# A decode step of gated attention and MLP: layer 1 and q with the weights stationary

## The chip, the cores and the metric

The kernel runs on one core of a Trainium2 chip. The metric is the device time of one execution in microseconds (us), given as the median of several runs. Executions of one kernel mostly agree within about 1% here, so differences below that are called equal unless said otherwise. Only runs that the record calls fast are used for ratios and verdicts; the medians given are over all runs of a sitting, the few slow ones included.

## The reference, cut to what matters

One token (D = 576) goes two ways, and a gate mixes the results:

```python
g = sigmoid((x * gate_w).sum(-1))
q = x @ wq                              # 576 -> 32 heads of 128
s = q . k   over the last 4096 keys     # 16 K/V heads, 2 q heads on each
o = softmax(s * 128**-0.5) @ v
a = o @ wo                              # 4096 -> 576
h = gelu(x @ w1 + b1)                   # 576 -> 4608, "layer 1"
b = h @ w2 + b2                         # 4608 -> 576
out = g * a + (1 - g) * b
```

Everything is bf16. There is one token, so every weight and every key and value is used once: 53.6 MB are read from HBM for very little arithmetic. K and V are 16.8 MB each, w1 and w2 5.3 MB each, wq and wo 4.7 MB each.

## The kernel before, where the change and the argument touch it

All large loads are issued in program order on one queue (SyncE's, "SPq" in the profile): w1, wq, eight K pairs (2 MB each, two heads), V pairs 0 to 2, half of w2, V pairs 3 to 7, wo, the rest of w2. K and V pairs share a ring of four buffers; a load into a used buffer waits until its reader is done.

A matmul on TensorE first loads one operand into the array (the stationary one) and then streams the other past it (the moving one). Layer 1 keeps x stationary and streams the weights past it. To place block b of the output on row b, the stationary operand is a window into a zero-padded copy of x. The result is four rows of 1152, which VectorE adds the bias to and TensorE turns into columns:

```python
for k in range(KM):                      # 4 slices of 128 input rows
    for b in range(NB):                  # NB = 4
        for c0, c1, dst in pieces:       # 512 + 512 + 128 columns
            nc.tensor.matmul(dst, lhsT=zx[:, k, 7 - b : 7 - b + NB],
                             rhs=w1_m[:, k, b * FB + c0 : b * FB + c1], ...)
# ... the last 64 input rows likewise
nc.vector.tensor_tensor(out=h_row[:], in0=h_ps, in1=b1_t[:], op=ALU.add)
for j in range(NJ):                      # fp32, a column of 128 from every 9th element
    nc.tensor.matmul(hacc[:, j * NB : (j + 1) * NB], lhsT=h_row[:, j:FB:NJ], rhs=ident_f[0:NB, 0:NB], ...)
# ... gelu on 128 x 36
```

q is done alike (36 matmuls of 512 columns, a cast, four transposing matmuls), then copied into the block-diagonal tile `qz`. Then comes the K loop, which the argument is about:

```python
for i in range(NPAIR):
    k_t = load_pair(A_k_cache, i)            # 4 buffers
    for c1 in range(2):
        kt = early[:, c1 * W : (c1 + 1) * W] # one half for each c1: the next pair's transpose
        nc.vector.transpose(out=kt..., in_=k_t[:, c1 * W : (c1 + 1) * W]...)  # frees k_t
        for j in range(4):
            for n in range(2):               # scores: need qz, free kt
                nc.tensor.matmul(s_ps[:, c1, n], lhsT=qz[:, i, j, :], rhs=kv[...], ...)
```

The transposes of pair 0 need no q. Those of pair 1 write where pair 0 lies, so they wait for pair 0's score matmuls, and those need q. The end of the kernel adds 64 half-rows of wo and 36 of w2 into one output row (`y_add`, two matmuls of 288 columns for each row; another 36 matmuls for the first half of w2 run earlier).

## Time and profile before

| | kernel before |
|---|---|
| median of the first 3 runs | 143.1 us |
| span of the profiled execution | 142.7 us |
| HBM read, mean over the span | 53.6 MB, 376 GB/s |
| TensorE matmul busy, VectorE busy | 72%, 37% |

The profiled run of the kernel before is slow (144.51 us), by a small margin.

In the profile PE stands for TensorE's matmuls, PEld for its weight loads, DVE for VectorE, ACT for ScalarE and POOL for GpSimd. The page's strips show the span in 40 slices of 3.57 us: VectorE's busy share in tenths, the share of the DMA engines, and the GB/s they moved.

```profile
...
DVE  3071003040049599999999476500000000100001
...
DMA  5999999999997398999999999999999999999600
GB/s 160 416 430 403 450 432 408 460 409 422 422 436 317 83 427 298 441 390 404 402 422 432 432 420 422 434 427 427 422 427 432 418 438 422 418 418 400 237 3 0
```

The stream moves about 425 GB/s in nearly every slice; it falls in the 13th, 14th and 16th slice and at the end. VectorE is mostly idle before the 13th slice (from 43 us) and nearly full after it. At 425 GB/s, 53.6 MB take 126 us, so a kernel with no hole in its stream would take 126 us and its two ends.

The same hole in the windows view (each row a stretch in us, then its length, busy time of the engines with instruction counts, the TensorE clock that the profile says was granted as a share of full speed, DMA share, GB/s):

```profile
...
core 0: us, PE busy (x) PEld busy (x) DVE busy (x) ACT busy (x) POOL busy (x), PEclk, DMA share, GB/s
...
46.00:48.00 2.00, 2.00 (x6) 0.72 (x5) 1.37 (x1) 0.00 (x0) 0.00 (x0) 0.50 0.04 16
48.00:50.00 2.00, 2.00 (x9) 0.81 (x8) 1.20 (x1) 0.00 (x0) 0.00 (x0) 0.82 0.71 147
54.00:56.00 2.00, 1.71 (x9) 0.67 (x8) 2.00 (x2) 0.00 (x0) 0.00 (x0) 1.00 0.66 197
44.00:68.00 24.00, 20.07 (x79) 7.93 (x79) 22.57 (x11) 0.00 (x0) 0.00 (x0) 0.93 0.84 330
...
```

From 44 to 68 us the mean is 330 GB/s. Against 425 that is 24 x (1 - 330/425) = 5.4 us lost. The waits of the DMA queue say who held it (us in total, number, longest):

```profile
...
engine line waited for: us in total, times, longest us
SPq L312 <- DVE early L333: 41.1, 8, 14.3
...
```

The longest of these waits, 14.3 us, is that of the fifth K load, the first one that needs a used buffer. It is issued here (start, length):

```profile
...
47.40 0.53 SPq L312 DMA_DIRECT2D kv_t<-in_A_k_cache_dram  x1
```

Why so late is in the timeline (start and length in us, engine, line, operation, count; in brackets the idle time before it and what ended it):

```profile
...
start us, us, engine line op out<-in xcount [idle before <-releaser]
...
23.72 1.35 DVE L221 TENSOR_TENSOR h_row<-hq_ps,b_t 4x1152 f32<-4x1152 f32 x1 [12.37 <-PE hq_ps L212]
...
25.12 4.45 PE L225 MATMUL hacc<-ident_f,h_row 4*128 4x4 f32 x18 [1.44 <-DVE h_row L221]
...
29.51 9.80 PE L260 MATMUL hq_ps<-wq_t,zx 128*8 128x512 bf16 x32
...
40.21 0.68 DVE L276 CAST q_r<-hq_ps 8x512 bf16<-8x512 f32 x1 [8.54 <-PE hq_ps L268]
...
42.87 4.51 DVE L333 STREAM_TRANSPOSE early<-kv_t 128x2048 f32<-128x2048 f32 x2
...
45.23 5.10 PE L339 MATMUL s_ps<-early 128*128 128x512 bf16 x15 [1.99 <-DVE early L333]
...
```

VectorE adds layer 1's bias at 23.7 us (L221), TensorE turns the rows (L225, 4.45 us), then streams q's weights (L260, 9.8 us), VectorE casts q at 40.2, and the first K transpose starts at 42.87, with no idle time before it. The first K pair had been in its buffer since about 33 us.

### The profile page before, as it was taken

The page shows a single profiled execution, that of the slowest core. Times are in us where ns is not written, and L with a number is a line of the kernel's source. Part 1 is how long each engine was busy: PE and PEld are TensorE (multiplying, and loading weights), DVE is VectorE, ACT ScalarE, POOL GpSimd, SP SyncE. Part 2 cuts the span into 40 slices and gives each one's busy share as a digit, 9 for nine tenths or more (in the row PEclk, how much of TensorE's full clock was granted, in tenths as well). Part 3 has the DMA queues.
Part 4 walks back from the last instruction along what each step waited for, and adds up shares of the span by engine and source line. Part 5 has one row for each costly group of instructions (what it writes and reads, how often), then busy time and mean ns, then how long its engine had stood idle before and what let it go on. Part 6 is the DMA issues. An engine that isn't in the chain of part 4 may idle for free.

```text
span 142.7 us, 2055 instructions
## 1 busy us (share of the span) xinstructions
PE 103.4 (72%) x922; PEld 56.0 (39%) x922; DVE 52.2 (37%) x71; ACT 6.8 (5%) x11; POOL 2.8 (2%) x13
## 2 busy tenths in 40 slices
PE   1049996999974979888898732999955055099992
PEld 1021342943421323333333212975745045055661
DVE  3071003040049599999999476500000000100001
ACT  3500000000000000000000006000000000000001
POOL 7000000000000000000000000000000000000000
PEclk9999999955998699999999995555995555556999
DMA  5999999999997398999999999999999999999600
GB/s 160 416 430 403 450 432 408 460 409 422 422 436 317 83 427 298 441 390 404 402 422 432 432 420 422 434 427 427 422 427 432 418 438 422 418 418 400 237 3 0
DMA packets 4344, 53.75 MB, mean 377 GB/s; under 512 B 488, under 2 KB 492, under 8 KB 1136
## 3 DMA queue, kind: packets, MB, share of 16 engines
q1 hardware_dynamic: 4322, 53.61, 90.4%
q8 instruction: 7, 0.11, 0.3%
q10 hardware_dynamic: 14, 0.01, 0.0%
q14 instruction: 1, 0.01, 0.0%
HBM read 53.62 MB, written 0.00 MB: 376 GB/s over the span
## 4 chain that ended last, share of the span: by engine, by line
PE 25%; DVE 24%; DMA 14%; issue 2%; ACT 1%; SPq 0%; DVEq 0%
DVE early L333 20%; DMA wo_t<-in_A_wo_dram 14%; PE ya_ps L190 8%; PE yb_ps L191 8%; PE o_ps L423 4%; PE s_ps L339 4%; DVE pt L381 2%; DVE m_466 L351 2%; ACT early L373 1%; PE t_ps L393 1%; SPq L312 0%; DVE mh L360 0%; PE mt_ps L356 0%; ACT out_row L459 0%; PE mb_ps L364 0%
## 5 line engine op out<-in xcount | busy, mean ns | idle before, releaser
L339 PE MATMUL s_ps<-early 128*128 128x512 bf16 x128 | 31.9, 393 | 6.5 <-DVE early L333 6.5
L333 DVE STREAM_TRANSPOSE early<-kv_t 128x2048 f32<-128x2048 f32 x16 | 35.3, 2278 | 1.5 <-PE s_ps L339 1.4
L423 PE MATMUL o_ps<-pt,kv_t 128*128 128x4 bf16 x512 | 14.8, 166 | 13.2 <-DMA kv_t<-in_A_v_cache_dram 10.2
L339 PEld LDWEIGHTS <-early 128*128 128x128 bf16 x128 | 12.6, 98 | 25.7 <-issue 12.8
L423 PEld LDWEIGHTS <-kv_t 128*128 128x128 bf16 x512 | 14.6, 103 | 13.8 <-DMA kv_t<-in_A_v_cache_dram 10.6
L202 PE MATMUL hq_ps<-w_t,zx 128*4 128x512 bf16 (+1 forms) x48 | 11.4, 405 | 6.1 <-DMA w_t<-in_B_w_dram 6.1
L190 PE MATMUL ya_ps<-wo_t,ov 128*1 128x288 bf16 x32 | 10.3, 346 | 3.0 <-DMA wo_t<-in_A_wo_dram 3.0
L190 PE MATMUL ya_ps<-w_t,gt 128*1 128x288 bf16 x36 | 11.0, 333 | 0.0
L191 PE MATMUL yb_ps<-w_t,gt 128*1 128x288 bf16 x36 | 11.0, 333 | 0.0
L442 DVE TENSOR_TENSOR om<-o_ps,rh 128x128 bf16<-128x128 f32 x1 | 0.3, 291 | 28.8 <-PE o_ps L423 28.8
L191 PE MATMUL yb_ps<-wo_t,ov 128*1 128x288 bf16 x32 | 10.3, 345 | 0.0
L260 PE MATMUL hq_ps<-wq_t,zx 128*8 128x512 bf16 x32 | 9.8, 482 | 0.0
L458 DVE CAST out_row<-ya_ps 1x288 bf16<-1x288 f32 x1 | 0.4, 446 | 18.0 <-PE ya_ps L190 18.0
L202 PEld LDWEIGHTS <-zx 128*4 128x4 bf16 x48 | 4.2, 99 | 6.8 <-issue 4.2
L221 DVE TENSOR_TENSOR h_row<-hq_ps,b_t 4x1152 f32<-4x1152 f32 x1 | 1.3, 1346 | 12.4 <-PE hq_ps L212 12.4
L260 PEld LDWEIGHTS <-zx 128*8 128x8 bf16 x32 | 3.3, 105 | 6.0 <-issue 3.8
L225 PE MATMUL hacc<-ident_f,h_row 4*128 4x4 f32 x18 | 4.5, 376 | 1.4 <-DVE h_row L221 1.4
L225 PEld LDWEIGHTS hacc<-ident_f,h_row 4*128 4x128 f32 x18 | 4.4, 330 | 1.8 <-DVE h_row L221 1.8
L191 PEld LDWEIGHTS <-ov 128*1 128x1 bf16 x32 | 3.2, 100 | 4.8 <-issue 2.7
L190 PEld LDWEIGHTS <-gt 128*1 128x1 bf16 x36 | 3.5, 97 | 2.2
L191 PEld LDWEIGHTS <-gt 128*1 128x1 bf16 x36 | 3.4, 96 | 2.2
L373 ACT ACTIVATE early<-s_ps,negm 128x1024 bf16<-128x1024 f32 x2 | 2.2, 1108 | 42.7 <-DVE negm L368 42.7
(88 smaller groups left out, 42.1 us busy)
## 6 DMA issues: line engine op xcount, KB each, us to landing
kv_t<-in_A_k_cache_dram SPq DMA_DIRECT2D x8, 2048.0 KB, 9.0
kv_t<-in_A_v_cache_dram SPq DMA_DIRECT2D x8, 2048.0 KB, 17.1
w_t<-in_B_w_dram SPq DMA_DIRECT2D x2, 2304.0 KB, 10.7
wo_t<-in_A_wo_dram SPq DMA_DIRECT2D x2, 2304.0 KB, 25.5
wq_t<-in_A_wq_dram SPq DMA_DIRECT2D x2, 2048.0 KB, 18.6
w_t<-in_B_w_dram SPq DMA_DIRECT2D x3, 1296.0 KB, 16.9
w_t<-in_B_w_dram SPq DMA_DIRECT2D x2, 576.0 KB, 21.6
wq_t<-in_A_wq_dram SPq DMA_DIRECT2D x1, 512.0 KB, 18.0
```

Source lines behind the costliest of these rows:

```text
L190: nc.tensor.matmul(ya_ps[:], lhsT=vec, rhs=row[:, 0:NH], start=start, stop=stop, skip_group_check=True)
L191: nc.tensor.matmul(yb_ps[:], lhsT=vec, rhs=row[:, NH:D], start=start, stop=stop, skip_group_check=True)
L202: nc.tensor.matmul(dst, lhsT=zx[:, k, 7 - b : 7 - b + NB], rhs=w1_m[:, k, b * FB + c0 : b * FB + c1], start=(k == 0 and b == 0), stop=Fals ...
L225: nc.tensor.matmul(hacc[:, j * NB : (j + 1) * NB], lhsT=h_row[:, j:FB:NJ], rhs=ident_f[0:NB, 0:NB], start=True, stop=True,)
L260: nc.tensor.matmul(q_ps, lhsT=zx[:, k, 7 - m : 7 - m + NQ], rhs=wq_m[:, k, m * 512 : (m + 1) * 512], start=(k == 0 and m == 0), stop=False,)
L333: nc.vector.transpose(out=kt.bitcast(FP32), in_=k_t[:, c1 * W : (c1 + 1) * W].bitcast(FP32))
L339: nc.tensor.matmul(s_ps[:, c1, n], lhsT=qz[:, i, j, :], rhs=kv[:, n, :, j // 2, :, j % 2], start=False, stop=(i == NPAIR - 1 and j == 3), ...
L351: nc.vector.reduce_max(out=m2[:, c1 : c1 + 1], in_=s_ps[:, c1].rearrange("p n k -> p (n k)"), axis=AX.X)
L373: nc.scalar.activation(out=p_x[:, c1 * 1024 : (c1 + 1) * 1024], in_=s_ps[:, c1].rearrange("p n k -> p (n k)"), func=ACT.Exp, bias=negm[:, ...
L381: nc.vector.transpose(out=pt[:, c1 * NCH : (c1 + 1) * NCH, :].rearrange("p c h -> p (c h)"), in_=p_x[:, c1 * 1024 : (c1 + 1) * 1024],)
L393: nc.tensor.matmul(t_ps[:], lhsT=ones_f[:], rhs=sl[:, c1, :], start=(c1 == 0), stop=(c1 == 1))
L423: nc.tensor.matmul(o_ps[:, 4 * i : 4 * i + 4], lhsT=v_t[:, c, :], rhs=pt[:, c, 4 * i : 4 * i + 4], start=(c == 0), stop=(c == 2 * NCH - 1),)
```

## The change

The intent: with one token the matmuls have one column of useful work. Let the weights be the stationary operand, 128 columns a load, and let x move, one column. Outputs then arrive as columns, which is the form that the rest needs: no transposing matmuls, no zero-padded copies, and the bias is added by VectorE on 128 x 36 instead of 4 x 1152 elements. To keep each w2 load's rows long, feature f = block, partition, j maps as before, with two blocks of 18 instead of four of 9, so layer 1's weight load takes every 18th column. w1 arrives in four pieces, whose rows are 9 KB, instead of two of 18 KB, and the first half of w2 in one load instead of two.

```diff
-    NB = 4
+    NB = 2
...
-    b1_t = const.tile([NB, FB], BF16, name="b1_t")
+    b1_t = const.tile([P, NB, NJ], BF16, name="b1_t")
...
-    for k in range(0, KM, 2):
-        nc.sync.dma_start(out=w1_m[:, k : k + 2, :], in_=w1_src[:, k : k + 2, :])
+    for k in range(KM):
+        nc.sync.dma_start(out=w1_m[:, k, :], in_=w1_src[:, k, :])
...
-    (layer 1 as above: 48 + 6 streaming matmuls, bias on rows, 9 fp32 transposing matmuls)
+    h_ps = ps_s.tile([P, NF], FP32, name="h_ps", tag="s")
+    for k in range(KM):
+        for c in range(NF):                       # NF = 36
+            f0 = (c // NJ) * FB + c % NJ
+            nc.tensor.matmul(
+                h_ps[:, c : c + 1],
+                lhsT=w1_m[:, k, f0 : (c // NJ + 1) * FB : NJ],   # NJ = 18
+                rhs=xt[:, k : k + 1],
+                ...
+            )
+    (the last 64 input rows: 18 matmuls of two columns)
+    nc.vector.tensor_tensor(out=hx[:], in0=h_ps[:], in1=b1_t[...], op=ALU.add)
...
-    (q as above: 32 + 4 streaming matmuls, cast, 4 transposing matmuls)
+    for k in range(KM):
+        for j in range(Hq):
+            nc.tensor.matmul(q_ps[:, j : j + 1], lhsT=wq_m[:, k, j * Dh : (j + 1) * Dh],
+                             rhs=xt[:, k : k + 1], ...)
+    (the last 64 input rows: 16 matmuls of two columns)
```

Above, lines in round brackets stand for code that is cut.

More of the change, by code (lines that the diff above doesn't have):

```diff
@@ L67 @@
     nc.scalar.dma_start(out=b2_row[:], in_=B_b2.rearrange("(o n) -> o n", o=1))
-    b1_t = const.tile([NB, FB], BF16, name="b1_t")
-    nc.scalar.dma_start(out=b1_t[:], in_=B_b1.rearrange("(o n) -> o n", o=NB))
+    b1_t = const.tile([P, NB, NJ], BF16, name="b1_t")
+    nc.scalar.dma_start(out=b1_t[:], in_=B_b1.rearrange("(b p j) -> p b j", b=NB, j=NJ))
     w1_t = big.tile([P, KM * F + FH], BF16, name="w1_t", tag="B")
@@ L144 @@
     )
-    zx = const.tile([P, KM, 15], BF16, name="zx")
-    nc.vector.memset(zx[:], 0.0)
-    zq = const.tile([P, 11], BF16, name="zq")
-    nc.vector.memset(zq[:], 0.0)
-    zh = const.tile([P, 5], BF16, name="zh")
-    nc.vector.memset(zh[:], 0.0)
-    nc.vector.tensor_copy(out=zx[:, :, 7], in_=xt_ps[:, 0:KM])
-    nc.vector.tensor_tensor(out=zq[:, 3:8:4], in0=xt_ps[:, 4:6], in1=par[:], op=ALU.mult)
-    nc.vector.tensor_copy(out=zh[:, 1:4:2], in_=zq[:, 3:8:4])
+    xt = const.tile([P, KM], BF16, name="xt")
+    nc.vector.tensor_copy(out=xt[:], in_=xt_ps[:, 0:KM])
+    xl = const.tile([P, 2], BF16, name="xl")
+    nc.vector.tensor_tensor(out=xl[:], in0=xt_ps[:, 4:6], in1=par[:], op=ALU.mult)
     junk_row = const.tile([1, D], BF16, name="junk_row")
@@ L193 @@
     y_add(one_f[0:1, 0:1], b2g[0:1, :], start=True)
-    hq_ps = ps_s.tile([P, 2048], FP32, name="hq_ps", tag="s")
-    h_ps = hq_ps[0:NB, 0:FB]
-    pieces = [(c0, min(c0 + 512, FB), h_ps[:, c0 : min(c0 + 512, FB)]) for c0 in range(0, FB, 512)]
+    h_ps = ps_s.tile([P, NF], FP32, name="h_ps", tag="s")
     for k in range(KM):
-        for b in range(NB):
-            for c0, c1, dst in pieces:
-                nc.tensor.matmul(
-                    dst,
-                    lhsT=zx[:, k, 7 - b : 7 - b + NB],
-                    rhs=w1_m[:, k, b * FB + c0 : b * FB + c1],
-                    start=(k == 0 and b == 0),
-                    stop=False,
-                    skip_group_check=True,
-                )
-    for b in range(NB // 2):
-        for c0, c1, dst in pieces:
-            nc.tensor.matmul(
-                dst,
-                lhsT=zh[:, 1 - b : 1 - b + NB],
-                rhs=w1_l[:, b * FB + c0 : b * FB + c1],
-                start=False,
-                stop=(b == NB // 2 - 1),
+        for c in range(NF):
+            f0 = (c // NJ) * FB + c % NJ
+            nc.tensor.matmul(
+                h_ps[:, c : c + 1],
+                lhsT=w1_m[:, k, f0 : (c // NJ + 1) * FB : NJ],
+                rhs=xt[:, k : k + 1],
+                start=(k == 0 and c == 0),
+                stop=False,
                 skip_group_check=True,
             )
-    h_row = const.tile([NB, FB], FP32, name="h_row")
-    nc.vector.tensor_tensor(out=h_row[:], in0=h_ps, in1=b1_t[:], op=ALU.add)
-    hacc = ps_o.tile([P, NF], FP32, name="hacc", tag="o")
     for j in range(NJ):
         nc.tensor.matmul(
-            hacc[:, j * NB : (j + 1) * NB],
-            lhsT=h_row[:, j:FB:NJ],
-            rhs=ident_f[0:NB, 0:NB],
-            start=True,
-            stop=True,
+            h_ps[:, j:NF:NJ],
+            lhsT=w1_l[:, j:FB:NJ],
+            rhs=xl[:, 0:2],
+            start=False,
+            stop=(j == NJ - 1),
+            skip_group_check=True,
         )
@@ L233 @@
     hx = const.tile([P, NF], FP32, name="hx")
-    nc.vector.tensor_copy(out=hx[:], in_=hacc[:])
+    nc.vector.tensor_tensor(
+        out=hx[:], in0=h_ps[:], in1=b1_t[:].rearrange("p b j -> p (b j)"), op=ALU.add
+    )
     z2 = const.tile([P, NF], FP32, name="z2")
@@ L244 @@
     nc.vector.reciprocal(out=e_h[:], in_=e_h[:])
-    gt = const.tile([P, NJ, NB], BF16, name="gt")
+    gt = const.tile([P, NF], BF16, name="gt")
     nc.vector.scalar_tensor_tensor(
-        out=gt[:].rearrange("p j b -> p (j b)"),
-        in0=hx[:],
-        scalar=omg[:, 0:1],
-        in1=e_h[:],
-        op0=ALU.mult,
-        op1=ALU.mult,
-    )
-    NQ = 8
-    q_ps = hq_ps[0:NQ, 1536:2048]
+        out=gt[:], in0=hx[:], scalar=omg[:, 0:1], in1=e_h[:], op0=ALU.mult, op1=ALU.mult
+    )
+    q_ps = ps_m.tile([P, Hq], FP32, name="q_ps", tag="m")
     for k in range(KM):
-        for m in range(NQ):
+        for j in range(Hq):
             nc.tensor.matmul(
-                q_ps,
-                lhsT=zx[:, k, 7 - m : 7 - m + NQ],
-                rhs=wq_m[:, k, m * 512 : (m + 1) * 512],
-                start=(k == 0 and m == 0),
+                q_ps[:, j : j + 1],
+                lhsT=wq_m[:, k, j * Dh : (j + 1) * Dh],
+                rhs=xt[:, k : k + 1],
+                start=(k == 0 and j == 0),
                 stop=False,
+                skip_group_check=True,
             )
-    for m in range(NQ // 2):
+    for j in range(Hq // 2):
         nc.tensor.matmul(
-            q_ps,
-            lhsT=zq[:, 3 - m : 3 - m + NQ],
-            rhs=wq_l[:, m * 512 : (m + 1) * 512],
+            q_ps[:, j : Hq : Hq // 2],
+            lhsT=wq_l[:, j * Dh : (j + 1) * Dh],
+            rhs=xl[:, 0:2],
             start=False,
-            stop=(m == NQ // 2 - 1),
-        )
-    q_r = const.tile([NQ, 512], BF16, name="q_r")
-    nc.vector.tensor_copy(out=q_r[:], in_=q_ps)
-    qt_ps = ps_m.tile([P, 4, NQ], FP32, name="qt_ps", tag="m")
-    for i in range(4):
-        nc.tensor.matmul(
-            qt_ps[:, i, :],
-            lhsT=q_r[:, i * Dh : (i + 1) * Dh],
-            rhs=ident[0:NQ, 0:NQ],
-            start=True,
-            stop=True,
+            stop=(j == Hq // 2 - 1),
+            skip_group_check=True,
         )
     q_b = const.tile([P, Hq], BF16, name="q_b")
-    nc.vector.tensor_copy(
-        out=q_b[:].rearrange("p (m i) -> p i m", i=4), in_=qt_ps[:]
-    )
+    nc.vector.tensor_copy(out=q_b[:], in_=q_ps[:])
     qj_ps = ps_o.tile([P, 4, NPAIR, 4], FP32, name="qj_ps", tag="o")
@@ L412, in y_w2 @@
         for j in range(NJ):
-            y_add(gt[:, j, b : b + 1], w2_t[:, b, j, :], stop=(b == NB - 1 and j == NJ - 1))
+            y_add(gt[:, b * NJ + j : b * NJ + j + 1], w2_t[:, b, j, :], stop=(b == NB - 1 and j == NJ - 1))
     for i in range(NPAIR):
         if i == 3:
-            for b in range(2):
-                load_w2(b, 0, NJ)
-            for b in range(2):
-                y_w2(b)
+            load_w2(0, 0, NJ)
+            y_w2(0)
         v_t = load_pair(A_v_cache, i)[:].rearrange("p (c d) -> p c d", d=Dh)
@@ L436 @@
         nc.sync.dma_start(out=wo_t[:, r : r + 16, :], in_=wo_src[:, r : r + 16, :])
-    for b, j0, j1 in [(2, 0, 9), (3, 0, 4), (3, 4, 7), (3, 7, 9)]:
+    for b, j0, j1 in [(1, 0, 9), (1, 9, 13), (1, 13, 16), (1, 16, NJ)]:
         load_w2(b, j0, j1)
@@ L453 @@
         y_add(ov[:, r : r + 1], wo_t[:, r, :])
-    for b in range(2, NB):
-        y_w2(b)
+    y_w2(1)
     out_row = const.tile([1, D], BF16, name="out_row")
```

## The prediction

> **What bounds it now.** The DMA stream. Median 143.1 us, profiled span 142.7; 53.6 MB are read. In the windows table the stream moves about 425 GB/s nearly everywhere (53.6 MB at 425 is 126 us). It stops once: from 45 us the one-microsecond windows show 180, 33, 0, 213, 82 GB/s; 54 to 56 us show 164 and 229. Against 425 GB/s that loses 4.9 us (45:56), or 5.4 us with the slightly low 56:68. The waits of the DMA queue say why: the fifth K load, issued at 47.4 us, waited 14.3 us for the transposes that free its buffer. In VectorE's program order those stand behind q: in the timeline the first K transpose starts at 42.87 us, although q's weights landed at about 27 us and the first K pair at about 32.
>
> Why q is late: TensorE works 8.9 to 23.6 us on layer 1 (54 moving matmuls), then bias 1.35 us, 18 fp32 transposing records 4.4 us, then q 29.5 to 40.2 us (36 matmuls), cast, transposes, copies. The tail (124.8 to 140 us) is TensorE-bound: 100 output-row matmuls, 24 at 0.24 us, the rest at 0.122.
>
> **What the change does.** Removes those 90 streaming matmuls, the 18 fp32 records, the 1.35 us bias, q_r and q's four transposes. Adds 162 + 144 pairs of a 128-column weight load and a one- or two-column matmul. The V stage has that form: 64 pairs in 1.70 us at full clock, 1.79 at half (27 to 28 ns). So q: 144 x 28 = 4.0 us. Layer 1's weights are read with a step of 36 bytes, which no bf16 load here has. The Trainium skill, "SBUF — State Buffer" (Door 1) says that each access to a new 16-byte line pays a penalty; no run here shows how much. The fp32 loads of h_row at 36-byte steps come every 243 ns, like contiguous fp32 ones (t_ps, about 0.25 us), so I estimate 30 to 120 ns: 5 to 19 us, against w1's arrival over 13 us. w1 lands in quarters, so work starts near 6 us. Layer 1 ends at 16 to 26 us, q at 28 to 31, just behind wq's landing.
> Bytes are unchanged; 9 KB rows should stream as now (w2's 10 KB rows do). b1 becomes 256 pieces of 36 bytes: off the path, under 0.5 us of stream.
>
> **On the critical path.** Only the gap counts. With q by 31 us the transposes (4.4 us per pair) keep up with arrivals (2.1 MB at 425: 4.93 us) and the stream stays full. V has four buffers and softmax (9.3 us after the last K matmul) leaves some 7 us of slack. All later stages shift by about 5 us; TensorE's tail follows wo's landing and stays about 15 us, plus or minus 1.5 with the clock's phase. The saved TensorE time itself (some 20 us) is mostly worth nothing.
> 143.1 - 5.1 = 138.0 us; 136.2 to 140.6 eight times in ten. Faster by over 2%: 0.89; within: 0.08; slower: 0.03.
>
> **What would show it.** No slice near 45 us under 390 GB/s; first K transpose at 30 to 34 us; K loads five to eight issued about 4.9 us apart; DVE waiting for K DMAs, not the reverse; wo's landing 5 us earlier; layer 1's pairs at 30 to 120 ns.
>
> **What would make it wrong.** Strided weight loads over about 175 ns a pair: then layer 1 passes 34 us, q 38.5, and the gap returns; over 240, slower. A colder TensorE clock in the K stage or tail (up to 2 us). The 36-byte b1 pieces slowing the stream.

## The result, and the profile after

| | before | changed |
|---|---|---|
| median, same chip, 4 runs each | 143.19 us | 137.85 us |
| range | 142.47 to 145.2 | 137.32 to 138.46 |
| ratio | | 0.9645 (0.9576 to 0.9713) |
| span of the profiled execution | 142.7 us | 136.1 us |
| mean GB/s, 44 to 68 us | 330 | 427 |

A ratio is the mean time of one kernel's fast runs over that of the other's of the same rounds, so it is not quite the ratio of the medians quoted; the bracket is its 95% interval. The 145.2 us run is left out of the ratio: without it the means are 142.9 and 137.9 us, 5.1 us apart, where the medians are 5.3 apart. The changed kernel is faster, by 3.6% (2.9 to 4.2%).

The strips of the changed kernel:

```profile
...
DVE  2152012012958999998894665000000000000001
...
DMA  4999999999999999999999999999999999999800
GB/s 114 423 422 423 432 433 414 433 414 433 424 433 419 419 438 419 438 414 443 414 438 421 424 424 462 394 424 428 419 433 414 433 416 428 427 424 406 344 34 0
```

The hole is gone; VectorE's busy stretch begins in the 11th slice (34 us), not in the 13th (43 us). The windows of the same stretches:

```profile
...
46.00:48.00 2.00, 1.71 (x9) 0.67 (x7) 2.00 (x2) 0.00 (x0) 0.00 (x0) 1.00 1.06 451
48.00:50.00 2.00, 1.70 (x8) 0.67 (x7) 2.00 (x2) 0.00 (x0) 0.00 (x0) 1.00 1.00 426
54.00:56.00 2.00, 1.71 (x9) 0.69 (x8) 2.00 (x2) 0.00 (x0) 0.00 (x0) 1.00 1.04 442
44.00:68.00 24.00, 19.60 (x83) 7.91 (x83) 22.93 (x12) 0.00 (x0) 0.00 (x0) 1.00 1.01 427
...
```

The queue's waits for the transposes are still there, eight of them, the longest now 6.0 us, and the fifth K load goes out at 37.8 us, while three earlier K pairs are still on their way:

```profile
...
SPq L276 <- DVE early L297: 33.9, 8, 6.0
...
```

```profile
...
37.84 0.54 SPq L276 DMA_DIRECT2D kv_t<-in_A_k_cache_dram  x1
```

And the timeline up to the first scores:

```profile
...
6.13 2.40 PE L194 MATMUL h_ps<-xt,w_t 128*128 128x1 bf16 x36 [3.26 <-DMA w_t<-in_B_w_dram]
...
13.91 4.63 PE L194 MATMUL h_ps<-xt,w_t 128*128 128x1 bf16 x72
...
18.40 1.26 PE L203 MATMUL h_ps<-xl,w_t 128*128 128x2 bf16 x18
19.70 0.20 DVE L213 TENSOR_TENSOR hx<-h_ps,b_t 128x36 f32<-128x36 f32 x1 [8.11 <-PE h_ps L203]
...
20.04 3.56 PE L285 MATMUL s_ps<-no_r,no_l 1*128 1x512 bf16 x8 [0.38 <-DVE hx L213]
...
23.54 1.87 PE L235 MATMUL q_ps<-xt,wq_t 128*128 128x1 bf16 x64
...
27.16 1.86 PE L235 MATMUL q_ps<-xt,wq_t 128*128 128x1 bf16 x64 [1.76 <-DMA wq_t<-in_A_wq_dram]
...
28.89 0.57 PE L244 MATMUL q_ps<-xl,wq_t 128*128 128x2 bf16 x16
...
31.02 0.26 ACT L267 CAST early<-qj_ps 32x128 bf16<-32x128 f32 x1 [0.35 <-DVE early L267]
...
33.31 4.50 DVE L297 STREAM_TRANSPOSE early<-kv_t 128x2048 f32<-128x2048 f32 x2 [2.32 <-DMA kv_t<-in_A_k_cache_dram]
35.67 8.21 PE L303 MATMUL s_ps<-early 128*128 128x512 bf16 x24 [5.67 <-DVE early L297]
...
```

Layer 1 (L194, L203) ends at 19.7 us instead of 23.7 with rows still to be turned, q's first half (L235) waits for nothing but its turn, its second half starts when its weights land (27.16 us), q ends at 29.5 us, and its copies are done at 31.3 us (43.1 us before). VectorE then idles 2.3 us and the first transpose waits for the K pair, not the reverse. The mask matmuls of the scores (L285, eight matmuls that write a mask into the accumulator of the scores) now run before q. Their code is unchanged; q no longer shares a PSUM tile with the scores, which is probably why the scheduler put them there.

The costliest groups of the new matmuls (busy us, mean ns of one, then idle before):

```profile
...
L194 PE MATMUL h_ps<-xt,w_t 128*128 128x1 bf16 x144 | 9.6, 201 | 3.7 <-DMA w_t<-in_B_w_dram 3.7
...
L235 PE MATMUL q_ps<-xt,wq_t 128*128 128x1 bf16 x128 | 3.7, 165 | 1.8 <-DMA wq_t<-in_A_wq_dram 1.8
...
```

The mean length of a record is latency, not cost: 36 pairs of layer 1 take 2.40 us, less one tail of 0.1 us, so a pair comes every 64 ns; 64 pairs of q take 1.87 us, so every 28 ns.

### The profile page after: what moved, and what is told of

The parts are those of the page before. It is cut to its first block, busy times and chain, and to the rows that moved or that the text cites. A ratio compares the mean times of both kernels' runs of the same rounds, so it can differ in the third digit from the quotient of the medians.

```text
span 136.1 us, 2436 instructions
## 1 busy us (share of the span) xinstructions
PE 92.2 (68%) x1116; PEld 57.9 (43%) x1116; DVE 50.4 (37%) x65; ACT 6.8 (5%) x11; POOL 2.8 (2%) x13
## 4 chain that ended last, share of the span: by engine, by line
DMA 49%; PE 27%; DVE 12%; issue 7%; ACT 1%; ACTq 1%; SPq 0%; DVEq 0%
DMA kv_t<-in_A_k_cache_dram 26%; DMA wo_t<-in_A_wo_dram 16%; PE ya_ps L184 8%; DMA b_t<-in_B_b_dram 8%; PE yb_ps L185 8%; DVE early L297 7%; PE s_ps L303 6%; PE o_ps L385 5%; DVE pt L345 2%; DVE m_661 L315 2%; ACT early L337 1%; PE t_ps L357 1%; SPq L276 0%; ACTq L63 0%; DVE mh L324 0%
## 5 line engine op out<-in xcount | busy, mean ns | idle before, releaser
L303 PE MATMUL s_ps<-early 128*128 128x512 bf16 x128 | 32.9, 404 | 11.3 <-DVE early L297 11.3
L385 PE MATMUL o_ps<-pt,kv_t 128*128 128x4 bf16 x512 | 15.0, 166 | 15.1 <-DMA kv_t<-in_A_v_cache_dram 10.8
L194 PE MATMUL h_ps<-xt,w_t 128*128 128x1 bf16 x144 | 9.6, 201 | 3.7 <-DMA w_t<-in_B_w_dram 3.7
L194 PEld LDWEIGHTS <-w_t 128*128 128x128 bf16 x144 | 9.3, 164 | 4.9 <-DMA w_t<-in_B_w_dram 3.9
L184 PE MATMUL ya_ps<-w_t,gt 128*1 128x288 bf16 x36 | 10.4, 320 | 0.0
L185 PE MATMUL yb_ps<-w_t,gt 128*1 128x288 bf16 x36 | 10.4, 319 | 0.0
L185 PE MATMUL yb_ps<-wo_t,ov 128*1 128x288 bf16 x32 | 9.7, 332 | 0.0
L185 PEld LDWEIGHTS <-ov 128*1 128x1 bf16 x32 | 3.1, 96 | 4.5 <-issue 2.7
L235 PE MATMUL q_ps<-xt,wq_t 128*128 128x1 bf16 x128 | 3.7, 165 | 1.8 <-DMA wq_t<-in_A_wq_dram 1.8
L235 PEld LDWEIGHTS <-wq_t 128*128 128x128 bf16 x128 | 3.6, 104 | 2.7 <-DMA wq_t<-in_A_wq_dram 1.8
L184 PEld LDWEIGHTS <-ov 128*1 128x1 bf16 x32 | 3.1, 97 | 2.4 <-DVE ov L412 0.4
L285 PE MATMUL s_ps<-no_r,no_l 1*128 1x512 bf16 x8 | 3.6, 620 | 0.4 <-DVE hx L213 0.4
```

The costliest lines, as they stand in the source:

```text
L184: nc.tensor.matmul(ya_ps[:], lhsT=vec, rhs=row[:, 0:NH], start=start, stop=stop, skip_group_check=True)
L185: nc.tensor.matmul(yb_ps[:], lhsT=vec, rhs=row[:, NH:D], start=start, stop=stop, skip_group_check=True)
L194: nc.tensor.matmul(h_ps[:, c : c + 1], lhsT=w1_m[:, k, f0 : (c // NJ + 1) * FB : NJ], rhs=xt[:, k : k + 1], start=(k == 0 and c == 0), sto ...
L235: nc.tensor.matmul(q_ps[:, j : j + 1], lhsT=wq_m[:, k, j * Dh : (j + 1) * Dh], rhs=xt[:, k : k + 1], start=(k == 0 and j == 0), stop=False ...
L285: nc.tensor.matmul(s_ps[:, n // 2, n % 2], lhsT=no_l[0:1, e, :], rhs=no_r[0:1, e, :], start=(e == 0), stop=False, skip_group_check=True,)
L385: nc.tensor.matmul(o_ps[:, 4 * i : 4 * i + 4], lhsT=v_t[:, c, :], rhs=pt[:, c, 4 * i : 4 * i + 4], start=(c == 0), stop=(c == 2 * NCH - 1),)
```

## The experiments

Theory: the whole gain is the hole in the stream, and the hole comes from late q, because K buffers can't be freed past pair 0 without it. Rival 1: the TensorE and VectorE time saved in layer 1 and q is itself on the path. Rival 2: the loads themselves became better, by the 9 KB rows. Every experiment was timed in three rounds beside the kernel before on the same chip. "Stall" below is 24 us x (1 - rate/425) from the windows row 44 to 68 us of the profiled run.

| run | rate 44:68 | stall | median us | over the changed kernel's 137.85 |
|---|---|---|---|---|
| before | 330 | 5.4 | 143.19 | 5.3 |
| changed | 427 | 0 | 137.85 | |
| b_bufs5 | 421 | 0.2 | 137.88 | 0.0 |
| b_earlyT | 330 | 5.4 | 144.3 | 6.5 |
| b_earlyT2 | 381 | 2.5 | 139.6 | 1.8 |
| only_q | 399 | 1.5 | 139.83 | 2.0 |
| only_h | 426 | 0 | 138.86 | 1.0 |
| a_delay4 | 425 | 0 | 137.46 | -0.4 |
| a_delay8 | 341 | 4.7 | 142.41 | 4.6 |
| a_delay10 | 290 | 7.6 | 146.73 | 8.9 |
| a_contig | 428 | 0 | 138.1 | 0.3 |
| a_w1pairs | 429 | 0 | 137.39 | -0.5 |
| a_bufs5 | 428 | 0 | 137.56 | -0.3 |
| a_ystat | 429 | 0 | 137.65 | -0.2 |

The runs come from several sittings, with the kernel before at 142.61 to 143.19 us beside them, so a few tenths in the last column mean nothing.

### b_bufs5: the old layer 1 and q, one more buffer

```diff
-    kv_pool = ctx.enter_context(tc.tile_pool(name="kv_pool", bufs=4, side="right"))
+    kv_pool = ctx.enter_context(tc.tile_pool(name="kv_pool", bufs=5, side="right"))
-    h_row = const.tile([NB, FB], FP32, name="h_row")
+    h_row = early[0:NB, 0 : 2 * FB].bitcast(FP32)
```

The second edit only makes room. 

> The kernel before with a fifth K/V buffer; layer 1 and q are untouched and stay late (q's copies end near 42.9 us). My theory (the whole gain is the stall of the DMA stream at 45 to 56 us, because late q keeps K buffers occupied): the fifth K load is issued long before 30 us, the stall disappears, about 138 us (137 to 139.5), ratio to before about 0.965. Rival (the TensorE and VectorE time saved in layer 1 and q is itself on the path): nothing of it is saved here, so 143 us, ratio 1.00.

Measured: correct, 137.88 us against 142.61, ratio 0.9702 (0.9621 to 0.9782). q's copies are as late as before, and the first transpose starts at 42.70 us. Its windows:

```profile
...
46.00:48.00 2.00, 2.00 (x6) 0.59 (x5) 1.20 (x1) 0.00 (x0) 0.00 (x0) 0.50 0.98 418
...
44.00:68.00 24.00, 20.19 (x80) 8.01 (x80) 22.55 (x11) 0.00 (x0) 0.00 (x0) 0.93 1.00 421
...
```

The longest wait of the queue is the same as before:

```profile
...
SPq L312 <- DVE early L333: 41.1, 8, 14.3
...
```

The same 14.3 us, now of the sixth load, cost nothing, because the stream had 2 MB more queued. The whole gain of the change is had without touching a matmul: rival 1 falls, and with it rival 2, since w1 and w2 are loaded as before here.

### only_q and only_h: each half of the change alone

only_q is the kernel before with the new q (and both forms of x); only_h is the changed kernel with the old q streamed.

```diff
 # only_q, against before
+    xt = ...; xl = ...            (beside zx, zq, zh)
-    (q streamed)
+    (q stationary)
 # only_h, against changed
+    zx = ...; zq = ...; zh = ...  (beside xt, xl)
-    (q stationary)
+    (q streamed, into its own bank)
```

> Layer 1 as before, q with the weights stationary. Theory: layer 1 ends near 29.5 us as before, q about 34 us, first K transpose near 35 us, fifth K load near 40 us: before the stream runs dry (about 45 us), so the full gain, 137.5 to 139 us. Rival: only q's part of the saved TensorE time, about half the gain, 140 to 141 us.

> Layer 1 with the weights stationary, q by moving weights as before. Theory: q waits for its weights (27 us) and then streams them, first K transpose at 35 to 39 us, fifth K load by 43 us: the full gain again, 137.5 to 139.5 us; the two halves don't add up. Rival: only layer 1's part, about half the gain, 140 to 141 us.

Measured: only_q 139.83 us, ratio 0.9838 (0.9768 to 0.9907); only_h 138.86 us, ratio 0.9768 (0.9712 to 0.9825), both correct. only_h is within the expectation. only_q misses it by about a microsecond and lies next to where the rival put it (140 to 141). Its trace says why it isn't the rival: its first K transpose starts at 38.65 us and not at 35, because the scheduler ran the mask matmuls (3.7 us) ahead of and amid q; so a small stall is left, 328 and 352 GB/s in 50:54, 1.5 us in all. The times alone don't tell a threshold from a sum: by the ratios of fast runs the halves save 1.6 and 2.3%, the whole change 3.6%, and the intervals leave room for both. The stalls do tell: with only half of the change, only_h has none left, and only_q has 1.5 of 5.4 us. About 0.5 us of each one's rest is the tail's clock: TensorE ran 5.7 and 5.6 us of it at half speed, against 4.7 us in the changed kernel, and the half-speed matmuls take twice as long (0.24 against 0.122 us), so half of the difference is lost. In only_q the first wo piece lands 2.45 us later than in the changed kernel, 0.9 us more than the rates account for; that is not traced.

### b_earlyT and b_earlyT2: only the order of two transposes

Both take the transposes of pair 0 in front of q's section in the kernel before. In the first the compiler's scheduler put them back behind q. In the second, two tiny copies tie the order:

```diff
+    k0_t = load_pair(A_k_cache, 0)
+    for c1 in range(2):
+        nc.vector.transpose(out=early[:, c1 * W : (c1 + 1) * W]..., in_=k0_t[...]...)
     ... (cut: q's matmuls)
     q_r = const.tile([NQ, 512], BF16, name="q_r")
+    for c1 in range(2):     # b_earlyT2 only; overwritten by the next line
+        nc.vector.tensor_copy(out=q_r[:, 8 * c1 : 8 * c1 + 8], in_=early[0:NQ, (c1 + 1) * W - 8 : (c1 + 1) * W])
     nc.vector.tensor_copy(out=q_r[:], in_=q_ps)
     ... (cut: the K loop takes k0_t for pair 0 and no longer transposes it)
```

> The kernel before with only the two transposes of the first K pair moved ahead of q's copies in VectorE's order (they need no q). Theory: the fifth K load is issued at 37 to 38 us instead of 47.4; the sixth still waits for the second pair, near 51 us, so a stall of 0 to 2 us stays; 138.5 to 140.5 us. Rival: 143 us.

Measured: 144.3 us, ratio 1.0135 (1.0061 to 1.021). The timeline shows the first transpose at 42.81 us, behind q's copies, so the edit never took place and the expectation was not tested. The run is still of use: its profiled execution counts as fast, and its stretch is that of the kernel before.

```profile
...
46.00:48.00 2.00, 2.00 (x6) 0.64 (x5) 1.31 (x1) 0.00 (x0) 0.00 (x0) 0.50 0.02 8
...
44.00:68.00 24.00, 20.15 (x80) 7.97 (x80) 22.60 (x11) 0.00 (x0) 0.00 (x0) 0.93 0.84 330
...
```

Why it is 1% slower than the kernel before stays open.

> The kernel before with the first K pair's two transposes truly ahead of q's copies on VectorE: the run b_earlyT left VectorE's order as it was, since the compiler's scheduler put the transposes behind q again, so it tested nothing. Here two tiny copies from the transposed tile into q_r (overwritten later) force the order, which the compiled instruction order confirms. Theory: first transpose near 33 us, fifth K load near 38 instead of 47.4 us; the sixth still needs q (K pair 1 can be transposed only when pair 0 was multiplied), so it stays at 51 to 53 us and a stall of 1 to 3 us remains: 139 to 141 us, 2 to 4 us faster than before. Rival (saved TensorE time is the gain): as before, 142.6 us.

Measured: correct, 139.6 us against 143.09, ratio 0.9821 (0.974 to 0.9902). The first transpose starts at 32.96 us; q's copies end at 42.3 us, little sooner than before. The stream holds until 50 us (418 GB/s in 48:50) and then shows 131 and 328 GB/s, when the second pair's buffer is missing; 2.5 us are lost. As the theory had it, moving pair 0 helps by one buffer's worth and the rest still hangs on q.

### a_delay4, a_delay10, a_delay8: the changed kernel with q held back

```diff
-    nc.vector.tensor_copy(out=q_b[:], in_=q_ps[:])
+    nc.vector.tensor_copy(out=scr[:, 0:Hq], in_=q_ps[:])
+    for _ in range(n):      # 128 x 1024 fp32, changes nothing
+        nc.vector.tensor_tensor(out=scr, in0=scr, in1=scr, op=ALU.max)
+    nc.vector.tensor_copy(out=q_b[:], in_=scr[:, 0:Hq])
```

`scr` is a tile of its own with n = 4 and 10; with n = 8 it lies in `early`, across the border of its halves, so that no transpose can go before it.

> The changed kernel with about 5 us of idle VectorE work (4 chained 128x1024 fp32 operations, estimated 1.2 us each) put between q's matmuls and q's copies. Theory: the first K transpose moves from 33.3 to about 36 us (2.3 us of the delay fall into the wait for the first K pair), the stream has slack until about 38.5 us, so nothing is lost: 137.5 to 138.7 us. Rival (q's end is itself on the path): 3 to 5 us later, 141 to 143 us.

> The same with 10 operations, about 12 us: first K transpose near 43 us, as in the kernel before (42.87 us). Theory: the stall comes back at 45 to 56 us with its size, and the time of the kernel before with it, 142 to 144 us, though layer 1 and q are the new ones. Rival (the saved TensorE time as such, or the DMA form of w1, is the gain): under 140 us.

> The changed kernel with q held back so that the K transposes can't slip ahead (in a_delay10 they did): 8 chained operations of 1.25 us on the tile that the transposes write. First transpose near 40 us, first score matmul near 45.5 us, as in the kernel before (45.2 us). Theory: the stall of the kernel before comes back, 3 to 6 us, 141 to 144 us, with all of the change's cheap TensorE work in place. Rival: under 140 us.

Measured: a_delay4 137.46 us, ratio 0.9646 (0.9588 to 0.9705): 5 us of delay (the four operations took 5.00 us) are free. a_delay10 146.73 us, ratio 1.028 (1.0205 to 1.0354): slower than expected, and slower than the kernel before. The scheduler slipped pair 0's transposes in among the ten operations, at 36.0 and 39.3 us, which pushed the end of q's copies to 48.3 us, against 43.1 in the kernel before; the stall came later (180, 0, 0, 66 GB/s in 50:58) and was larger, 7.6 us. a_delay8 is the cleaner repeat: its first score matmul starts at 45.33 us, as in the kernel before (45.23), and it takes 142.41 us against 143.09, ratio 1.0007 (0.994 to 1.0074):

```profile
...
50.00:54.00 4.00, 3.04 (x14) 1.24 (x13) 4.00 (x3) 0.00 (x0) 0.00 (x0) 1.00 0.39 160
54.00:56.00 2.00, 1.70 (x9) 0.67 (x7) 2.00 (x2) 0.00 (x0) 0.00 (x0) 1.00 0.73 205
44.00:68.00 24.00, 19.94 (x80) 7.95 (x81) 20.27 (x11) 0.26 (x1) 0.00 (x0) 1.00 0.86 341
...
```

The kernel has all of the change's cheap TensorE work and none of its gain. Here, too, pair 0's transposes went early, at 40.0 and 42.4 us, so most of the stall sits at 50 to 56 us; it is 4.7 us, against 5.4 in the kernel before. That the times agree to 0.1% is partly luck, since the tails differ: in the profiles TensorE ran the first 3.1 us of the tail at half speed here and 5.9 us in the kernel before.

### a_w1pairs and a_bufs5: the 9 KB rows, and a fifth buffer on top

a_w1pairs takes back the `for k in range(KM)` loads of w1; a_bufs5 is the changed kernel with `bufs=5`.

> The changed kernel with w1 loaded as before, two 18 KB pieces of rows a partition instead of four of 9 KB. Layer 1 starts at about 9 us instead of 6 and ends 0 to 3 us later; q is tied to the landing of its own weights. Expected: no difference in time (within 0.5%), 137.5 to 138.5 us. Rival (the finer rows make the stream or the start better): 139 us or more.

> The changed kernel with a fifth K/V buffer. Theory: the changed kernel has no stall left that buffers could hide, so 137.3 to 138.3 us, the same. Rival (fifth buffer and early q are two separate gains): 3 us or more faster, 133 to 135 us.

Measured: 137.39 us, ratio 0.9657 (0.9581 to 0.9734), and 137.56 us, ratio 0.9679 (0.9623 to 0.9734), against 143.09 on the same chip; both correct. The 9 KB rows gain nothing. In the first 2 us of the span the stream of a_w1pairs moved 111 GB/s and that of a_bufs5, with four smaller loads, 47; that is worth 2 x (111 - 47)/425 = 0.3 us and too little to show. A fifth buffer and an early q are two cures of one stall.

### a_contig: layer 1 from neighbouring columns (a wrong result)

```diff
-                lhsT=w1_m[:, k, f0 : (c // NJ + 1) * FB : NJ],
+                lhsT=w1_m[:, k, c * P : (c + 1) * P],
-            lhsT=w1_l[:, j:FB:NJ],
+            lhsT=w1_l[:, j * P : (j + 1) * P],
```

> Wrong result on purpose: the changed kernel with layer 1's weight loads of 128 neighbouring columns instead of every 18th. Expected: a pair takes 28 ns instead of 64, as q's pairs do; layer 1 is then bound by w1's arrival and ends 1 to 3 us sooner; the time stays within 0.5% of the changed kernel's, since layer 1's end is off the path. Rival: the step matters for the time, 2 us or more faster.

Measured: wrong, as meant (relative error 0.19), and 138.1 us, ratio 0.9688 (0.9623 to 0.9753). TensorE's timeline of layer 1:

```profile
...
6.23 1.12 PE L194 MATMUL h_ps<-xt,w_t 128*128 128x1 bf16 x36 [3.37 <-DMA w_t<-in_B_w_dram]
...
13.38 1.12 PE L194 MATMUL h_ps<-xt,w_t 128*128 128x1 bf16 x36
...
16.14 0.64 PE L203 MATMUL h_ps<-xl,w_t 128*128 128x2 bf16 x18 [0.30 <-DMA w_t<-in_B_w_dram]
...
```

36 pairs take 1.12 us, so 28 ns a pair, against 64 with the step of 36 bytes; layer 1 ends at 16.8 us instead of 19.7. The time is that of the changed kernel: layer 1 is not on the path.

### a_ystat: the same trick for w2 and wo

```diff
 def y_add(vec, row, start=False, stop=False):
-    nc.tensor.matmul(ya_ps[:], lhsT=vec, rhs=row[:, 0:NH], ...)
-    nc.tensor.matmul(yb_ps[:], lhsT=vec, rhs=row[:, NH:D], ...)
+    for m, d0 in enumerate([0, 128, 256, 384, 448]):
+        nc.tensor.matmul(yt_ps[:, m : m + 1], lhsT=row[:, d0 : d0 + P], rhs=vec, ...)
 ... at the end: copy yt_ps, one fp32 matmul against the identity (5 x 128), cast, two small stores
```

> The same trick where TensorE does end last: w2 and wo stationary too (five 128-column weight loads a row, out in five columns, turned to rows by one small fp32 matmul). The tail of the changed kernel is 14.7 us of TensorE after wo lands at 118.8 us, while the stream ends near 129.5. Expected: a wo or w2 row costs 5 x 28 = 140 ns at either clock instead of 245 to 480, so TensorE finishes within 0.5 us of the last landing (about 131 us); copy, turn and copy add some 0.8 us against today's one copy; the span falls by 1 to 2.5 us, to about 136 us. If the tail is bound by the last landing already, nothing is gained.

Measured: correct, 137.65 us, ratio 0.9648 (0.9595 to 0.9701): no gain over the changed kernel, against my expectation of 136. The tail:

```profile
...
128.71 2.08 PE L185 MATMUL yt_ps<-gt,w_t 128*128 128x1 bf16 x65 [0.72 <-DMA w_t<-in_B_w_dram]
...
131.15 0.56 PE L185 MATMUL yt_ps<-gt,w_t 128*128 128x1 bf16 x15 [0.36 <-DMA w_t<-in_B_w_dram]
...
131.88 0.43 PE L185 MATMUL yt_ps<-gt,w_t 128*128 128x1 bf16 x10 [0.18 <-DMA w_t<-in_B_w_dram]
132.35 0.16 DVE L426 COPY y_sb<-yt_ps 128x5 f32<-128x5 f32 x1 [16.29 <-PE yt_ps L185]
...
132.57 0.59 PE L428 MATMUL yr_ps<-ident_f,y_sb 128*5 128x128 f32 x2 [0.26 <-DVE y_sb L426]
133.19 0.28 DVE L430 CAST out_row<-yr_ps 5x128 bf16<-5x128 f32 x1 [0.68 <-PE yr_ps L428]
...
```

TensorE waits for weights between its bursts and is done 0.4 us after the last w2 piece, as hoped. But that piece came at 131.88 us, and copy, matmul and cast then take until 133.47 (133.19 + 0.28). The changed kernel casts its output at nearly the same moment:

```profile
...
133.38 0.45 DVE L419 CAST out_row<-ya_ps 1x288 bf16<-1x288 f32 x1 [17.37 <-PE ya_ps L184]
```

In the changed kernel TensorE works from 118.82 us to there, and its trace has the last landing of a weight at 130.66 us. So of those 14.6 us all but 2.7 (133.38 - 130.66) hide behind the stream. a_ystat had that much to gain, but its own last landing came 1.2 us later, and its last burst and the turning of the result took the other 1.6 us (133.47 - 131.88). The loads of the two kernels are the same; at 130.0 to 131.5 us the kept traces show 9, 0 and 0 GB/s in the changed kernel and 65, 25 and 18 in a_ystat. Why its stream ended later is not traced.

No version tried beats the changed kernel clearly. With its stream full from 4 to 128 us, what is left above 126 us is the start and the end.

## Why the prediction was right

- The time, 138.0 predicted and 137.85 measured, and the mechanism. The hole of 5.4 us is about the gain (5.3 us by the medians, 5.1 by the fast runs); b_bufs5 gets it without the new matmuls, and a_delay8 loses it with them.
- First K transpose at 30 to 34 us: it starts at 33.31. K loads five to eight about 4.9 us apart: they go out at 37.8, 44.5, 48.9 and 53.3 us, so only roughly; what matters is that each is queued in time. VectorE waits for K pairs, as foreseen, at four places.
- q in 144 x 28 ns: the pairs came at 28 ns. Layer 1 at 30 to 120 ns a pair: 64. The Trainium skill, "SBUF — State Buffer" (Door 1), says an access that crosses to a new 16-byte line pays a penalty; a_contig measures what the step costs this load, 64 against 28 ns, which agrees, and shows that it is off the path. No run tried other steps, so that the 16-byte line is the reason is not shown. My ground for the upper end, the fp32 loads at the same step, was no measure of it.
- The threshold. I gave 38.5 us as the latest harmless end of q. only_h, whose copies end at 37.7 us, keeps the stream full; only_q, at 38.9 us, loses 1.5 us. a_delay4 ends them at 38.5 us and loses nothing, though one of its first two transposes slipped ahead of them. So the limit is about where I put it, but three runs don't fix it to a few tenths: what the stream lacked in only_q was the sixth K load, which went out at 49.15 us (47.69 in only_h), and that load also hangs on the pace of pair 0's score matmuls.
- wo lands 6.0 us earlier in the profiles (124.80 to 118.82), 5 predicted; the spans differ by 6.6, since TensorE's half-speed part of the tail was 4.7 us instead of 5.9. The before profile is of a run called slow, so the median's 5.3 us is the number to use.
- Not foreseen, and harmless: b1 in 36-byte pieces took 10.6 us to land, and the queue waited 5.0 us for that before it issued the first K load at 12.48 us. Some 5 MB were still queued then (10.0 MB of w1 and wq, less 10.8 us at 425 GB/s).
- One reading was too simple: "the tail is TensorE-bound". TensorE works there without a break, but in the changed kernel the last landing is only 2.7 us before its end (3.4 us in the kernel before), and a_ystat, which needs far less of TensorE there, is no faster. A busy stretch at the end of the chain of waits is not what its removal is worth.

## What to carry to other kernels

In a kernel bound by its stream, cheaper arithmetic off the two ends is worth what it brings forward the time at which buffers come free, and only up to the point where the stream no longer runs dry: find the hole, follow the queue's longest wait to the instruction that frees the buffer, and ask what stands before that instruction in its engine's order. The test that separates the causes is to cure the wait in another way (one more buffer) and to put the delay back with the new code in place. After such an edit, look at the compiled order: in five of the twelve runs here (b_earlyT, only_q and the three delays) the scheduler moved something that the test relied on, in one so that it tested nothing.

## What the Trainium skill lacked or had wrong

- "TensorE: Matmul & The Clock Gate" (Back-to-back issue gap) gives a floor of about 25 ns between the starts of matmuls of up to 64 columns, but neither there nor under LDWEIGHTS a figure in bf16 for a stream of 128-column loads each with a one-column matmul. Here such a pair comes every 28 ns from neighbouring columns, close to that floor. It barely depends on the clock: the weight loads of 64 pairs of the V stage (kernel before) took 1.67 us where the windows view reads a clock of 1.00, and 1.79 where it reads 0.50.
- The same page has no cost for weight loads from strided columns, and the SBUF page's penalty no size: a step of 36 bytes in bf16 takes 64 ns a pair instead of 28.
- "TensorE: Matmul & The Clock Gate" (Part 1) puts the warm-up near 3.4 us of activity; in the tails of these profiles TensorE ran continuously for 2.8 (a_bufs5) to 5.9 us (before) at half speed first. With the stationary form (a_ystat) the windows view reads a granted clock of 0.50 from 80 us to 133 us, and its pairs still come every 28 ns. That column is no sure sign of pace: in the changed kernel it reads 1.00 from 36 to 41 us, while the 512-column matmuls there come every 0.43 us, the pace that goes with 0.50 in the kernel before (46 to 48 us).
- "SBUF — State Buffer" (Summary) says to estimate loads from HBM at about 358 GB/s; this one core held 425 GB/s. "Perfetto Trace Analysis" (Roofline), with about 435 GB/s for a lone core, agrees with the traces.
